# An mLSTM cell and a leaky-ReLU feed-forward on one core: the first chunk's order of work written anew, weight quarters loaded in four transfers

## The chip, the cores and the metric

The kernel runs on one core of a Trainium2 chip. A core has five engines that run side by side and wait for one another by semaphores: TensorE (PE; its weight loads are listed as PEld), VectorE (DVE), ScalarE (ACT), GpSimd (POOL) and SyncE (SP), which issues nearly all transfers (DMAs). Each engine works through its own queue in order. The metric is device time in microseconds, lower is better.

## The reference

```python
# mLSTM cell: 4 batches, 8 heads, 768 steps, head size 40
for t in range(S):
    m_new = np.maximum(f[t] + m, i[t])
    f_stab, i_stab = np.exp(f[t] + m - m_new), np.exp(i[t] - m_new); m = m_new
    C = f_stab * C + i_stab * einsum('bhd,bhe->bhde', v[t], k[t])
    n = f_stab * n + i_stab * k[t]
    h = einsum('bhde,bhe->bhd', C, q[t]); nq = einsum('bhd,bhd->bh', n, q[t])
    y[t] = sigmoid(o[t]) * h / np.maximum(np.abs(nq), 1)
# feed-forward: x is y as (3072, 320); w_in (320, 2048), w_out (2048, 320)
h = x @ w_in
out = np.maximum(0.01 * h, h) @ w_out
```

The inputs of the cell are float32. w_in and w_out come as float64, 8 bytes an element.

## The kernel before

**Tiling.** The 768 steps are cut into 6 chunks of 128. A chunk has one item for each of the 4 batches, so items ("s") count from 0 to 23, and items 0 to 3 are the first chunk. Inside a chunk the recurrence is written as products: the gates become running sums (`gates`), a matrix of decays w for each head (mask by `spread_first`, exponential by `prep_exp`), scores k·q by `u_scores`, and the values by `u_values`; the state at a chunk's end comes from `state`. The feed-forward of a chunk (512 tokens) starts when its cell is done and runs beside the next chunk's cell.

**The first chunk.** It has no earlier state and no earlier feed-forward to run beside. An item passes through: loads of k, q, v (`load`) and o (`load_o`), transposes of k and q by TensorE into PSUM and a copy by ScalarE (`u_transpose`), scores, multiplication by w on VectorE, the state product, which needs v scaled by GpSimd (`prep_vu`), and its copy on VectorE (`u_state`), values, denominators and gate on VectorE with a last product on GpSimd (`gate`), transposes of the result and five copies on ScalarE (`u_x`), which place it for the feed-forward. `prepare_step` is three memsets on GpSimd that ready the item's state tile for the next chunk.

**The weights.** w_in is loaded in four quarters (`load_weights` 0 to 3), each as float64 words into a raw area, and narrowed to float32 by `narrow_weights`: one step on ScalarE (L247) and six on VectorE (L249 to L263). w_out follows in eight pieces. Each quarter's 320 rows are kept in five slots of 64 rows, in two halves: row half r = 0 in partitions 0 to 63, r = 1 in 64 to 127, and `SLOTS` says which 64 rows stand in which slot. The halves use different slot orders, so that the products of a feed-forward half (`half` in `ff_units`) run in pairs on different rows of TensorE.

**What sets the order.** The whole program is traced with TensorE, VectorE, ScalarE and GpSimd in the order in which the code calls the operations; SP's transfers come out in program order here too. `first_chunk` is written out by hand: it calls the steps of items 0 to 3 one after the other, and with them two halves of the first feed-forward (`ffs[0]`, `ffs[1]`: tokens of items 0 and 1). After it a few more loads are issued (items 4 and 5, weights, items 6 and 7), and a loop runs the rest: the remaining feed-forward halves, between them the units of the next chunk's cell at fixed places. In the loop's first turn `ahead(4)` puts item 4's transposes (`u_split`, tiles tk, L534) on TensorE, which need its k and q, and then `ffs[2]`, which needs the tokens of items 2 and 3. Below, "ff 0", "ff 1" and "ff 2" are the first three halves, "q 4" is q of item 4.

**PSUM.** Two pools of four banks each: `psf` (feed-forward, masks, and the warming products) and `psc` (everything else of the cell). A new tile waits until a bank of its pool is read out.

**Warming.** `warm(14)` issues 14 products of the identity with itself on TensorE at the start. Nothing reads them.

Of the kernel before, what the change touches and what calls it, by code (L numbers as in the profile page):

```python
# [18 lines left out]
def kernel(  # L19
# [184 lines left out]
    def load_weights(n):  # L204

        m = n - QN
        if n < QN:
            dst = w_in[:, n, :]
        else:
            dst = w_out[:, 2 * m : 2 * m + 2, :].rearrange("p a d -> p (a d)")  # L210
        to = dst
        if wide:
            if n < 2:
                at = NF * GT - 2 * WC * (n + 1)
                raw = acts_l[:, at : at + 2 * WC].bitcast(U64)
            elif n < QN:
                raw = raw_t[:, WC * (n - 2) : WC * (n - 1)]
            elif m < 2:
                raw = w_out[:].rearrange("p f d -> p (f d)")[:, (2 + m) * WC : (3 + m) * WC].bitcast(U64)
            else:  # L220
                at = (4, 0, 1, 2, 3, 4)[m - 2] * HW
                raw = raw_t[:, at : at + HW]
            raws[n] = (raw, dst)
            to = raw
        if n < QN:
            src = moe_w_in[:, n * QC : (n + 1) * QC].rearrange("(k p) (r c) -> r p k c", p=DP, r=2)
            for slot in range(KC):
                for r in range(2):
                    nc.sync.dma_start(
                        to[DP * r : DP * (r + 1), 2 * P * slot : 2 * P * (slot + 1)], src[r, :, SLOTS[r][slot], :],  # L230
                    )
        else:
            rows = moe_w_out[2 * m * P : 2 * (m + 1) * P, :]
            nc.sync.dma_start(to.rearrange("p (a d) -> p a d", d=Dm), rows.rearrange("(a p) d -> p a d", p=P))
# [190 lines left out]
    def spread_first(a, s2):  # L425


        ab = [psf.tile([P, 2, H // RG, P], F32, name=f"ab{r}", tag="mm") for r in range(RG)]
        for n in range(2):
            for m in range(H // RG):  # L430
                for r in range(RG):
                    bh = (s2 + n) * H + m * RG + r
                    rows = ts(r, BH)
                    nc.tensor.matmul(
                        ab[r][:, n, m, :], lhsT=ident[rows, r * BH + bh : r * BH + bh + 1].to_broadcast([BH, P]),
                        rhs=a[rows, :], start=True, stop=True,
                    )
        for n in range(2):
            w = st[s2 + n]["w"] = wk.tile([P, H, P], F32, name="w", bufs=NL)
            for r in range(RG):  # L440
                nc.vector.tensor_tensor(
                    w[:, r::RG, :], ab[r][:, n], cmask[:].unsqueeze(1).to_broadcast([P, H // RG, P]), op=ALU.add,
                )
# [98 lines left out]
    def u_transpose(s):  # L542
        d = st[s]
        d["kqT"] = wk.tile([P, 2, PR * P], F32, name="kqT")
        for i in range(2):
            tp = psc.tile([P, PR, P], F32, name="tkq", tag="c")
            for j in range(PR):
                nc.tensor.transpose(  # L548
                    tp[:, j, :], d["kq"[i]][:, 2 * j : 2 * j + 2, :].rearrange("p h d -> p (h d)"), ident[:],
                )  # L550
            nc.scalar.copy(d["kqT"][:, i], tp[:].rearrange("p j t -> p (j t)"))

    def u_scores(s):
        d = st[s]
        kqT, w = d["kqT"], d["w"]
        sc = [psc.tile([P, PR, P], F32, name=f"sc{r}", tag="c") for r in range(2)]
        for j in range(PR):
            for r in range(2):
# [3 lines left out]
                )  # L562
        for r in range(2):
            nc.vector.tensor_tensor(w[:, r::2, :], w[:, r::2, :], sc[r][:], op=ALU.mult)
# [62 lines left out]
    def u_state(s):  # L627
        state(s)
        state_copy(s)

# [6 lines left out]
    def u_values(s):  # L637
        d = st[s]
        pa = d["pa"] = psc.tile([P, H, D1], F32, name="pa", tag="c")
        for h in range(H):  # L640
            nc.tensor.matmul(pa[:, h, :], lhsT=d["w"][:, h, :], rhs=d["va"][:, h, :D1], start=True, stop=True)  # L641
        d["den"] = wk.tile([P, H], F32, name="den")
        denominators(d["den"][:], pa[:, :, D])

    def gate(s):
# [7 lines left out]
        )  # L653
        nc.gpsimd.tensor_tensor(x3, x3, d["den"][:].unsqueeze(2).to_broadcast([P, H, D]), op=ALU.mult)
# [78 lines left out]
    def u_x(s):  # L733
# [3 lines left out]
        if b == 0:  # L737
            st["xT", c] = wk.tile([P, KC, GT], F32, name="xT", bufs=1)
        xT = st["xT", c]
        xt = psc.tile([P, KF + 1, P], F32, name="xt", tag="c")  # L740
        for kk in range(KF):
            nc.tensor.transpose(xt[:, kk, :], d["x"][:, ts(kk, P)], ident[:])
        nc.tensor.transpose(xt[:KR, KF, :], d["x"][:, KF * P :], ident[:])
        tok = ts(b, P)
# [5 lines left out]
        del st[s]  # L750
# [149 lines left out]
    def cell_units(c):  # L900
        if c == 1:
            units = [(fn, c * B + n) for n in range(B) for fn in (u_parts, u_plain)]
            units.insert(2 * B - 2, (u_gates, c + 1))
            return units + [(u_x, s) for s in range(B, 2 * B)]
# [39 lines left out]

    def first_chunk():

        for n in range(B):
            load(n)
        load_o(0)
        load_o(1)  # L950
        load_weights(0)
        load_o(2)
        load_o(3)
        for n in range(1, 3):
            load_weights(n)
        gates(0)
        gates_exp(0)
        warm(14)
        bu, a, _ = bus[0]
        gates_T(0, bu)  # L960
        u_transpose(0)
        spread_first(a, 0)
        run(prep_exp(0))
        prep_vu(0)
        prep_vu(1)
        prepare_tiles()
        u_transpose(1)
        u_scores(0)
        u_state(0)
        run(prep_exp(1))  # L970
        spread_first(a, 2)
        gates(1)
        gates_exp(1)
        u_scores(1)
        u_values(0)
        u_state(1)
        u_transpose(2)
        prep_o(0)
        gate(0)
        run(prep_exp(2))  # L980
        prep_vu(2)
        w = narrow_weights(0)
        next(w, None)
        u_values(1)
        u_gates(1)
        u_scores(2)
        prep_o(1)
        gate(1)
        u_state(2)
        for _ in w:  # L990
            pass
        u_transpose(3)
        run(prep_exp(3))
        prep_vu(3)
        prepare_step(0)
        prepare_step(1)
        u_x(0)
        u_values(2)
        u_scores(3)
        u_x(1)  # L1000
        u_state(3)
        prep_o(2)
        gate(2)
        w = narrow_weights(1)
        for _ in range(4):
            next(w, None)
        ffs = ff_units(0)
        ffs[0]()
        u_values(3)
        prep_o(3)  # L1010
        gate(3)
        u_x(2)
        ffs[1]()
        for _ in w:
            pass
        u_x(3)
        prepare_step(2)
        prepare_step(3)
        return ffs

    E = mybir.EngineType
    with tc.manual_schedule(engines={E.PE, E.DVE, E.Activation, E.Pool}):
        ffs = first_chunk()
        for s in (B, B + 1):
            feed(s)
            for i in range(1, 3):
                load_late(s, i)
            if s == B:
                load_weights(3)
        for n in range(3):  # L1030
            load_weights(QN + n)
        for s in (B + 2, B + 3):
            feed(s)


        ffs = ffs[2:]
# [98 lines left out]
```

## Time and profile before

| | |
|---|---|
| median of 3 runs | 509.8 us (506.64 to 511.63) |
| the profiled execution, span | 508.0 us; what lies around the span isn't recorded |
| PE busy in the span | 492.0 us (97%) |
| DVE, ACT, POOL busy | 308.1, 171.5, 137.7 us |
| first chunk: last transposes of its results on PE | 49.18 to 49.7 us |
| mean granted clock | 0.983 |

The page cuts the span into 40 slices of 12.7 us. A digit is the busy share of an engine in tenths, and PEclk the granted TensorE clock in tenths of full speed. A line of the timeline reads: start, duration, engine, line of the kernel, operation, output<-inputs, count, and in brackets the idle time before it and what ended it. "SPq" is SP's queue: the time is that of issuing. A DMA in the chain of work has the time from its issue to its landing. In a table of windows a row gives a stretch, its length, each engine's busy time with a count of instructions (PE, PEld, DVE, ACT, POOL), the granted clock, the DMA engines' busy share and GB/s.

### The profile page before, as it was taken

The numbers are of one execution on the slowest core, as the hardware profiler recorded it, in microseconds if no ns is written. First come the engines' busy times: TensorE is split into PE (matmuls) and PEld (weight loads), VectorE is DVE, ScalarE is ACT, GpSimd is POOL, SyncE is SP. The second block draws the span as 40 slices with busy tenths as digits, with TensorE's granted clock in tenths as the row PEclk, the third lists the DMA queues.
The fourth block names the chain that finished last, engine by engine and source line by source line (L and its number), as shares of the span: only waits on it lengthen the run. The fifth ranks groups of instructions, "written<-read, shape, count | busy, mean of one in ns | idle before, by whom it ended". The sixth has DMA issues, their size and how long they took to land.

```text
span 508.0 us, 12526 instructions
## 1 busy us (share of the span) xinstructions
PE 492.0 (97%) x4981; PEld 366.6 (72%) x4981; DVE 308.1 (61%) x515; ACT 171.5 (34%) x478; POOL 137.7 (27%) x175
## 2 busy tenths in 40 slices
PE   8878999999999999999999999999899999999997
PEld 7766878767655489955589855599755599744797
DVE  4779898899954778635765826764825664101321
ACT  3664864652722510323411323311213411022210
POOL 4243443360402404413104614014612003000020
PEclk9877999999999999999999999999999999999999
DMA  9977687888765551565663566564466212200001
GB/s 116 146 204 154 149 219 185 168 152 175 155 145 87 131 124 46 133 130 144 147 132 92 115 137 170 137 141 97 109 135 177 68 53 62 69 1 1 1 1 52
DMA packets 165290, 59.21 MB, mean 117 GB/s; under 512 B 128816, under 2 KB 156016, under 8 KB 165232
## 3 DMA queue, kind: packets, MB, share of 16 engines
q1 hardware_dynamic: 164848, 58.28, 52.2%
q8 instruction: 39, 0.64, 0.5%
q14 instruction: 19, 0.16, 0.1%
q10 hardware_dynamic: 384, 0.13, 0.1%
HBM read 51.68 MB, written 6.70 MB: 115 GB/s over the span
## 4 chain that ended last, share of the span: by engine, by line
PE 79%; DVE 9%; DMA 3%; ACT 3%; POOL 2%; issue 2%; SPq 2%; ACTq 0%; POOLq 0%; DVEq 0%
PE ph L759 36%; PE po L835 26%; PE po L794 6%; PE pT L695 3%; PE sd L614 3%; SPq L359 1%; PE sd L619 1%; DMA S<-in_v_dram 1%; ACT kqT L540 1%; PE tkq L548 1%; DVE raw L261 1%; DMA rb<-in_q_dram 1%; DMA w<-a_dr 1%; PE pa L641 1%; DVE qn L511 1%
## 5 line engine op out<-in xcount | busy, mean ns | idle before, releaser
L759 PE MATMUL ph<-xT,w_in 64*128 64x512 f32 (+1 forms) x1120 | 216.2, 538 | 2.4 <-DVE y L887 1.4
L759 PEld LDWEIGHTS ph<-xT,w_in 64*128 64x128 f32 x1120 | 108.6, 189 | 95.1 <-issue 86.3
L767 ACT ACTIVATE acts<-ph 128x512 f32<-128x512 f32 (+1 forms) x112 | 53.9, 533 | 179.0 <-PE ph L759 178.9
L835 PEld LDWEIGHTS po<-w_out,acts 128*128 128x128 f32 x640 | 87.3, 190 | 3.8 <-issue 3.8
L835 PE MATMUL po<-w_out,acts 128*128 128x160 f32 x640 | 89.1, 300 | 0.0
L450 POOL TENSOR_TENSOR w<-w,i 128x512 f32<-128x512 f32 x20 | 26.9, 1345 | 117.3 <-DMA w<-a_dr 117.2
L624 DVE TENSOR_TENSOR qn<-w,sd 64x512 f32<-64x512 f32 x40 | 27.4, 684 | 40.2 <-PE sd L619 20.5
L458 ACT ACTIVATE w<-w,gT 128x64 f32<-128x64 f32 (+1 forms) x192 | 50.8, 348 | 2.7 <-POOL w L450 1.7
L592 POOL TENSOR_TENSOR S<-S,f 40x336 f32<-40x336 f32 x36 | 32.0, 889 | 67.3 <-PE pT L695 36.3
L835 PE MATMUL po<-raw,acts 128*128 128x160 f32 x320 | 45.5, 300 | 0.0
L835 PEld LDWEIGHTS po<-raw,acts 128*128 128x128 f32 x320 | 43.9, 190 | 0.3
L794 PE MATMUL po<-w_out,acts 128*128 128x320 f32 x128 | 36.5, 436 | 0.0
L702 DVE STREAM_TRANSPOSE hb<-pT 128x512 f32<-128x512 f32 x16 | 11.5, 717 | 31.0 <-PE pT L695 30.8
L794 PEld LDWEIGHTS po<-w_out,acts 128*128 128x128 f32 x128 | 23.6, 190 | 9.3 <-issue 0.3
L511 DVE TENSOR_TENSOR qn<-kqT,ea 64x512 f32<-64x512 f32 x32 | 28.4, 888 | 1.0
L709 POOL TENSOR_TENSOR xb<-xb,den 128x320 f32<-128x320 f32 x16 | 11.7, 729 | 56.8 <-DVE xb L706 56.6
L596 DVE TENSOR_TENSOR S<-S,sd 40x336 f32<-40x336 f32 x36 | 18.1, 503 | 12.1 <-POOL S L592 11.2
L614 PEld LDWEIGHTS sd<-kqT 40*64 40x64 f32 x640 | 19.9, 135 | 6.1 <-issue 6.1
L822 DVE TENSOR_TENSOR raw<-acts 128x1024 f32<-128x1024 f32 x10 | 11.8, 1222 | 18.3 <-ACT acts L767 18.2
L713 DVE STREAM_TRANSPOSE x<-xb 128x512 f32<-128x512 f32 x16 | 18.2, 1140 | 7.6 <-POOL xb L709 7.6
L835 PE MATMUL po<-raw 128*128 128x160 f32 x160 | 22.5, 299 | 0.0
L835 PEld LDWEIGHTS po<-raw 128*128 128x128 f32 x160 | 22.0, 190 | 0.0
(151 smaller groups left out, 551.8 us busy)
## 6 DMA issues: line engine op xcount, KB each, us to landing
w<-a_dr SPq DMA_DIRECT2D x40, 128.0 KB
rb<-in_k_dram SPq DMA_DIRECT2D x64, 80.0 KB
rb<-in_q_dram SPq DMA_DIRECT2D x64, 80.0 KB
rb<-in_o_gate_dram SPq DMA_DIRECT2D x64, 80.0 KB
ea<-a_dr SPq DMA_DIRECT2D x32, 128.0 KB
kn<-in_k_dram SPq DMA_DIRECT2D x24, 160.0 KB
raw<-in_moe_w_out_dram SPq DMA_DIRECT2D x6, 640.0 KB
S<-in_v_dram SPq DMA_DIRECT2D x80, 40.0 KB
```

The lines of the kernel that those rows point to most:

```text
L450: nc.gpsimd.tensor_tensor(w, w, cm2.unsqueeze(1).to_broadcast([P, H, SL]), op=ALU.add)
L458: yield nc.scalar.activation(w[:, h, :], w[:, h, :], AF.Exp, bias=gT[c][:, 0, bh : bh + 1], scale=1.0)
L511: nc.vector.tensor_tensor(mixed(s)[rows, 1 - r], d["kqT"][rows, 1].rearrange("p (h t) -> p h t", t=SL), d["ea"][rows], op=ALU.mult,)
L592: nc.gpsimd.tensor_tensor(new, old, g, op=ALU.mult)
L596: nc.vector.tensor_tensor(new, new, st[s]["dC", u], op=ALU.add)
L614: nc.tensor.matmul(bank[1 - u][toks, h, :], lhsT=kqT[rows, 0, ts(h, SL)], rhs=kqT[rows, 1, ts(h, SL)], start=True, stop=True,)
L624: nc.vector.tensor_tensor(mixed(s)[toks, u], w[toks], bank[1 - u][toks], op=ALU.mult)
L713: nc.vector.transpose(in_blocks(xq[:]), xb[:].rearrange("p (j n) d -> p j n d", n=TB))
L759: nc.tensor.matmul(ph[r][:, cols], lhsT=w_row(r, slot, j), rhs=xT[DP * r : DP * (r + 1), slot, cols], start=(slot == 0), stop=(slot == KC ...
L767: nc.scalar.activation(acts[:, f, cols], ph[r][:, cols], AF.Prelu, alpha=0.01)
L794: nc.tensor.matmul(po[n][:], lhsT=acts[:, f, ts(n, P)], rhs=w_out[:, f, :], start=(f == 0), stop=(f == NF - 1),)
L835: nc.tensor.matmul(bank[:], lhsT=left[:, f, :], rhs=right[:, f, :], start=f == 0, stop=f == KH - 1)
```

## The change

1. `first_chunk` no longer calls the steps in Python order. A string `ORDER` lists them, 131 entries with the transfers, and a loop runs them. To let parts of a step stand apart, helpers are split: `u_transpose` (one set at a time) and `transpose_copy`, `u_scores` and `scores_mix`, `spread_first` and `spread_mask`, `state` and `state_copy`, `u_values` and `values_den`, `gate` and `gate_scale`, `u_x` and `x_copy`. The operations are the same ones.
2. The transfers are in that list too. Weight quarter 0 (`lw 0`) goes ahead of item 3's k, q, v (`ld 3`), o of item 3 (`lo 3`) behind quarter 2. The loads of items 4 to 7 (`fd`), of q and o of items 4 and 5 (`ll`), and of weights 3 to 6 are in the list; o of item 4 goes ahead of q of item 4, and q and o of item 5 behind weights 3 to 5 and item 6.
3. The warming products are 9 and not 14; `idle n` adds n products of the same kind further on, 14 in all, into a PSUM tile of their own (`warmer`).
4. A quarter of w_in is loaded by four transfers and not ten: for each half, one of three slots and one of two.

```diff
-            for slot in range(KC):
-                for r in range(2):
+            for r in range(2):
+                at = 0
+                while at < KC:
+                    k0, m = run_of(r, at)
                     nc.sync.dma_start(
-                        to[DP * r : DP * (r + 1), 2 * P * slot : 2 * P * (slot + 1)], src[r, :, SLOTS[r][slot], :],
+                        to[DP * r : DP * (r + 1), 2 * P * at : 2 * P * (at + m)].rearrange("p (k c) -> p k c", k=m),
+                        src[r, :, k0 : k0 + 2 * m - 1 : 2, :],
                     )
+                    at += m
...
+    def warmer():
+        st["warm"] = psf.tile([P, P], F32, name="warm", tag="mm")
+
+    def idle(n):
+        for _ in range(n):
+            nc.tensor.matmul(st["warm"][:], lhsT=ident[:], rhs=ident[:], start=True, stop=True)
+
+    ORDER = """
+warm 9; g 0; ld 0; ge 0; ld 1; tr 0 0; ld 2; tr 0 1
+ug 0; lo 0; tc 0 1; ab 0; abw 0; tr 1 0; tr 1 1; lo 1
+lw 0; vu 0; tc 0 0; vu 1; exp 0; tc 1 1; abw 1; ld 3
+exp 1; lo 2; warmer; sc 0; tiles; st 0; lw 1; scm 0
+stc 0; tc 1 0; ab 2; val 0; st 1; g 1; abw 3; abw 2
+sc 1; o 0; lw 2; ge 1; idle 2; idle 1; stc 1; o 1
+scm 1; idle 3; tr 2 0; tc 2 0; lo 3; tr 2 1; nw 0; tc 2 1
+ug 1; nw 0; val 1; vu 3; den 0; gate 0; vu 2; gate 1
+sc 2; tr 3 0; nw 0; exp 2; den 1; scm 2; ps 0; st 2
+gp 0; exp 3; tc 3 0; tr 3 1; x 0; tc 3 1; idle 4; sc 3
+nw 0; gp 1; stc 2; xc 0; x 1; nw 0; val 2; nw 0
+o 2; nw 0; st 3; scm 3; xc 1; nw 1; gate 2; nw 1
+ff 0; o 3; val 3; den 2; nw 1; ps 1; fd 4; gp 2
+stc 3; den 3; gate 3; ll 4 2; ll 4 1; ps 2; gp 3; nw 1
+x 2; xc 2; ps 3; fd 5; ff 1; lw 3; nw 1; lw 4
+x 3; lw 5; nw 1; fd 6; ll 5 1; xc 3; ll 5 2; lw 6
+idle 4; nw 1; fd 7
+"""
...
+            "ld": load, "lo": load_o, "lw": load_weights, "g": gates, "ge": gates_exp, "warm": warm,
+            "ug": lambda c: gates_T(c, bus[c][0] if c == 0 else bus.pop(c)[0]),
+            "tr": u_transpose, "tc": transpose_copy, "ab": lambda n: spread_first(bus[0][1], n), "abw": spread_mask,
+            "exp": lambda n: run(prep_exp(n)), "vu": prep_vu, "tiles": prepare_tiles, "sc": u_scores, "scm": scores_mix,
+            "st": state, "stc": state_copy, "val": u_values, "den": values_den, "o": prep_o, "gate": gate,
+            "gp": gate_scale, "nw": step, "ps": prepare_step, "x": u_x, "xc": x_copy, "ff": ff,
+            "warmer": warmer, "idle": idle, "fd": feed, "ll": load_late,
```

## The prediction

> **What bounds the kernel now.** I read the page's slices first, then the windows by stage, then the timelines of TensorE and of the transfer queue, then the chain.
>
> ```profile
> PE   8878999999999999999999999999899999999997
> PEclk9877999999999999999999999999999999999999
> DMA  9977687888765551565663566564466212200001
> ```
>
> From the fifth slice on (50 us) PE is busy nearly throughout at the full clock. Only the first four slices, which are the first chunk, have idle PE and a reduced clock. So whatever moves the start of the steady stage moves the end by about as much. That start is the third half of the first feed-forward (ff 2), at 51.64 us:
>
> ```profile
> 38.33 0.79 PE L572 MATMUL dC<-vu,kn 128*40 128x42 f32 x16 [1.80 <-ACT xT L749]
> 39.77 4.64 PE L759 MATMUL ph<-xT,w_in 64*128 64x256 f32 x20 [0.66 <-DVE w_in L263]
> 46.82 2.43 PE L759 MATMUL ph<-xT,w_in 64*128 64x256 f32 x20
> 50.62 0.25 PE L534 MATMUL tk<-ident,rb 64*40 64x64 f32 x2 [0.65 <-DMA rb<-in_q_dram]
> 51.64 4.59 PE L759 MATMUL ph<-xT,w_in 64*128 64x256 f32 x40
> ```
>
> ff 0 waits until 39.77 for the last narrowing step of weight quarter 0 (L263), and takes 4.64 us where ff 1 takes 2.43. Then PE waits 0.65 us for q of the next chunk's batch 4. The windows show the clock (after the colon: length, PE busy, ..., granted clock, DMA share, GB/s):
>
> ```profile
> 17.51:20.93 3.42, 1.84 (x29) 1.50 (x28) 3.35 (x12) 0.97 (x4) 0.00 (x0) 1.00 0.83 132
> 24.35:31.17 6.82, 6.69 (x52) 6.07 (x51) 2.48 (x8) 3.05 (x7) 0.87 (x3) 0.50 0.72 179
> 34.59:37.99 3.40, 0.68 (x7) 0.28 (x3) 3.33 (x3) 2.65 (x10) 2.32 (x5) 1.00 0.62 199
> 41.41:44.82 3.41, 3.41 (x19) 2.33 (x15) 3.27 (x7) 0.38 (x2) 1.14 (x1) 0.50 0.65 126
> ```
>
> After a stretch with PE 54% busy (17.51) and one with 20% (34.59) the clock is 0.50, until a stretch is full.
>
> The transfer queue (SP), and q's own landing in the chain:
>
> ```profile
> 18.77 7.75 SPq L229 DMA_DIRECT2D acts<-in_moe_w_in_dram  x10
> 27.83 6.58 SPq L229 DMA_DIRECT2D acts<-in_moe_w_in_dram  x10
> 34.45 6.35 SPq L229 DMA_DIRECT2D raw<-in_moe_w_in_dram  x10
> 46.77 3.46 DMA rb<-in_q_dram
> ```
>
> The three quarters that are fetched before q 4 take 20.7 us of SP, and q 4 lands at 46.77 + 3.46 = 50.2.
>
> **The change, part by part.**
>
> *Transfers.* A quarter is 128 x 1280 x 8 bytes = 1.31 MB. Issued as ten it moves at an issue each 0.64 us. As four, SP issues it in about 4 x 0.64 = 2.6 us, so the transfers' own rate decides. The trace has no such transfer, and these are the nearest rows:
>
> ```profile
> 29.70:31.50 1.80, 1.79 (x9) 1.48 (x9) 0.92 (x3) 1.72 (x4) 0.03 (x1) 0.59 0.89 255
> 34.40:40.90 6.50, 2.78 (x33) 2.06 (x31) 6.30 (x9) 4.83 (x12) 2.46 (x6) 0.78 0.65 208
> 65.40:67.70 2.30, 2.30 (x24) 1.84 (x20) 2.23 (x3) 0.66 (x2) 1.24 (x1) 1.00 0.93 298
> ```
>
> At 29.7 pieces of w_in that were issued earlier run off a backlog, at 255 GB/s: 5.1 us a quarter. At 34.4 they come at the pace of the issues, 208 GB/s: 6.3. At 65.4 w_out comes in 128-partition transfers of 0.66 MB with rows of 2.5 KB, 298 GB/s and the best to hope for: 4.4. At the bad end, if a transfer to 64 partitions gets half of that, 149 GB/s: 8.8. I take 5.1, from the row with the same packets and a queue behind them. Then three quarters take 15.3 us, and 0.6 for one late issue such as SP shows now and then, 15.9 in place of 20.7: 4.8 saved. The o of batch 4 now goes ahead of q 4: one issue, 0.6 us. q 4 lands at 50.2 - 4.8 + 0.6 = 46.0. From its landing to ff 2 are 51.64 - 50.24 = 1.4 us (the rest of the tk transposes), so **by the transfers ff 2 starts at 47.4**.
>
> A rule of the Trainium skill speaks against this part. The Trainium skill, page "SBUF — State Buffer", section "Door 1: The DMA port swizzle", says that 64 neighbouring partitions reach only 8 of the 16 DMA ports, about 218 GB/s at best. By that, the new order, which fills one half of the partitions with two transfers and then the other (ten transfers alternated), takes 6.0 us a quarter, an estimate from the page's figure, and q 4 lands at 48.7. The 255 GB/s row alternates halves and so doesn't refute it.
>
> *The order.* Quarter 0 moves ahead of batch 3's k, q and v. It lands at 29.1 now: the narrowing's first step on ACT (L247) starts at 29.12 after a wait for it. Three transfers of 160 KB leave its front, at SP's pace of 1.18 us each, and it takes 5.7 instead of 7.75 itself: 29.1 - 3.5 - 2.1 = 23.5. Batch 1's v lands at 12.55; five transfers (k, q, v 2, o 0, o 1) later it is 18.5, then come quarter 0 (5.7) and k, q, v 3 (3.5): v 3 lands at 27.7, some 7 us later than now. On ACT that first step now stands ahead of batch 2's second transpose copy and of exp 2 and 3: they wait with it for the quarter, from 21.7, and exp 3 is done at 30.4, before anything asks for it.
>
> To find where that leads I went down each engine's new queue with the rows' durations, every step at the later of its engine's end and its last input. PE: transposes 0.5 us a set, scores 1.14, state 0.46, values 1.85, x 0.4, ff half 2.38; a spare is two passes of 0.107 (four 128-wide weight loads of tkq take 0.42). DVE: mask 1.37, mix 1.28, gate 0.49, narrowing 0.83 + 1.24 + 1.50 + 0.87 + 1.50 + 1.49. ACT: exp 2.45, x copies 1.66. POOL: vu 0.95, product 0.74, step memsets 1.08. The same walk down the old queues, with the granted clock, ends at 49.6; in the trace the last x transposes run from 49.18 to 49.7.
>
> Until 18.8 us old and new are alike, since both wait for k, q and v. Nine warming products instead of fourteen end at 5.3, and PE then waits for k till about 6.7: nothing lost, unless the clock rises 3.4 us later for it (0.6 at most). The six spares at 18.8 to 20.1 fill the wait of 1.58 us after which the old clock fell. Then POOL binds: its queue has vu 3 ahead of vu 2, and vu 3 needs v 3. So 27.7 + 0.95 + 0.95 = 29.6, state 2 follows on PE after 2.3 us without work, then memsets 1.08 and the product 0.74, and x 0 starts at 31.6. From there PE has, with no gap over 0.1, x 0.4, four spares 0.86, scores 1.14, x 0.4, values 1.85, state 0.46, ff 0 2.38, values 1.85, x 0.4, ff 1 2.38, x 0.4, four spares 0.86: 13.4 us, end **45.0**, against 49.7. ff 0 falls at 36.7, just where quarter 0's narrowing ends on DVE (36.6). The last x copies end on ACT at 46.3 (51.5 now), quarter 1's narrowing on DVE at 48.2 (51.8).
>
> No spare stands in the gap ahead of state 2. By the 54% row such a gap lets the clock fall for one or two stretches of 3.4 us; at a pace of 0.53 (ff 0's 2.43 to 4.64) the walk then ends 0.4 or 1.9 us later, the x copies at 46.7 or 48.2. The Trainium skill, page "TensorE: Matmul & The Clock Gate", section "What's actually happening", has the clock fall after at least one idle window of 3.4 us; by that the gap would cost nothing. The row at 17.51 shows a fall after a window that was half busy, and the row decides.
>
> *Sum.* ff 2 starts at the later of 47.4 (q 4) and 46.4 to 48.3 (x copies). I take 47.7, 3.9 us before 51.64. Splitting the helpers in two adds no instruction. The spares' 14 x 0.214 = 3.0 us of PE are counted: 1.3 in an old wait, 0.9 within the 13.4 on the path, the last 0.9 beside the wait for q 4 and the x copies. With that cover gone they cost 0.9 more.
>
> What is late next: DVE, which waits 1.2 us for ACT at 52.98 now, moves along. q of batch 5 now stands behind w_in quarter 3, two of w_out and two batches' k, v and w (4.4 us each on SP): 42.5 + 4.4 + 5.1 + 4.2 + 4.4 + 3.5 = 64.1, and is needed at 68.8 - 3.9 = 64.9. That hides it by 0.8 us; at slower quarters its lateness adds to PE.
>
> The profiled execution spans 508.0, no more is shown around it; the median of the runs is 509.8, 1.8 above. 508.0 - 3.9 = 504.1 on its account, **506.0** on the median's.
>
> **The rivals.**
>
> *Quick quarters.* At 4.4 us three take 13.8, q 4 lands at 43.9 and no longer decides; v 3 comes 0.7 us earlier, the x copies end at 45.6. If the clock holds, ff 2 starts at 45.7, 5.9 earlier: 503.9. For it: 298 GB/s. Against: 64 partitions, not 128.
>
> *Half the partitions bind.* At no better than the 208 GB/s row, 6.3 us, three take 19.5, q 4 lands at 49.6, ff 2 starts at 51.0. PE then has 2 to 3 us without work ahead of tk, and perhaps a stretch at 0.50 behind it (1.6 us): between 0.6 gained and 1.0 lost, 509 to 511. The Trainium skill's 6.0 would give ff 2 at 50.1, 508.3.
>
> *Slower than before.* At 149 GB/s, 8.8 us, three take 27.0, q 4 lands at 57.1, ff 2 starts at 58.5: 6.9 lost, 517. The loss begins at 6.9 us a quarter. Against it: the small ones reach 208 GB/s into the same halves.
>
> *It doesn't keep the clock.* With the old stretches at 0.50 the walk ends at 48.4 on PE and 49.7 on ACT, ff 2 starts at 50.0: 1.6 gained, 508.2. For it: the gap ahead of state 2.
>
> **How the numbers follow.** Forecast (504.7 to 507.5) 0.40; quick 0.27; half the partitions 0.18; slower 0.08; clock 0.07. 1% of the time is 5.1 us, about what a measurement can tell from no change. Faster by over 1% (under 504.7) is the quick case and the forecast's low edge: 0.34. Slower by over 1% is the slow case, and a little of the half-partition one with q 5 late as well: 0.10. The rest is 0.56. The range leaves out the slow case and the outer edges of the others: 502.8 to 511.0.
>
> **What would show it.** SP's w_in rows at 2.6 to 5 us a quarter; ACT's first step of narrowing near 23.5; POOL's vu 3 near 27.7 after a wait for v; ff 0 near 36.7, in 2.4 us; the last x near 44; tk's wait for q 4; ff 2 near 47.7. The forecast is wrong if quarters take over 6 us, if the wait for q 4 is over 2 us or gone, if POOL's vu isn't what state 2 waits for, or if the steady stage gives the gain back in waits for w_in quarter 3, q 5 or DVE.

## The result, and the profile after

| | before | after | ratio |
|---|---|---|---|
| median of 20 runs each | 510.33 us | 513.5 us | 1.006 [1.004, 1.008] |
| profiled execution, span | 508.0 us | 512.0 us | |

The changed kernel is slower by 0.6%, 3.2 us by the medians. The forecast was a gain, to 506.0 us, with a range from 502.8 to 511.0. A "mark" below is the start of a piece of work on TensorE (PE) in the profiled execution.

The slices of the page, after:

```profile
PE   6876989999999999999999999999799999999997
PEclk9979799999999999999999999999999999999999
DMA  9999887788653551565664467664466312100001
```

The DMA row is now 9 in each of the first four slices, and the clock has a low slice of its own at the fifth (51 to 64 us), where before the steady stage was already running at full clock. The timeline of PE, after (the lines that answer to those of before; start, duration, then in brackets the wait):

```profile
28.05 2.08 PE L570 MATMUL sc<-kqT 40*128 40x128 f32 x16 [3.60 <-ACT kqT L561]
...
38.48 2.43 PE L785 MATMUL ph<-xT,w_in 64*128 64x256 f32 x20 [0.18 <-DVE w_in L267]
...
46.84 0.44 PE L757 MATMUL xt<-ident,x 128*128 128x128 f32 x2 [1.22 <-POOL x L672]
51.73 0.33 PE L541 MATMUL tk<-ident,rb 64*40 64x64 f32 x2 [3.20 <-DMA rb<-in_q_dram]
53.59 8.57 PE L785 MATMUL ph<-xT,w_in 64*128 64x256 f32 x60
...
73.40 0.25 PE L541 MATMUL tk<-ident,rb 64*40 64x64 f32 x2 [1.31 <-DMA rb<-in_q_dram]
```

The first chunk did get shorter: its last transposes start at 46.84 and not 49.18. But behind them PE waits 3.20 us for q 4 (0.65 before), so ff 2 starts at 53.59 and not 51.64. The 60 products from its start on take 8.57 us; in a run below, at full clock, they take 6.75. Then comes a new wait of 1.31 us for q 5, ahead of the next item's transposes (tk again). The windows, after (length, PE, PEld, DVE, ACT, POOL busy, granted clock, DMA share, GB/s):

```profile
23.20:26.60 3.40, 1.25 (x12) 1.13 (x11) 0.00 (x0) 0.42 (x1) 0.00 (x0) 1.00 1.02 107
...
30.00:40.00 10.00, 9.77 (x102) 8.65 (x102) 9.76 (x15) 8.72 (x24) 5.84 (x9) 0.83 1.07 213
44.00:47.00 3.00, 1.78 (x17) 1.27 (x14) 2.65 (x3) 2.46 (x8) 2.05 (x2) 1.00 0.35 34
47.07:50.48 3.41, 1.45 (x15) 1.18 (x13) 3.34 (x3) 2.96 (x6) 1.85 (x4) 1.00 0.82 176
50.48:53.88 3.40, 2.15 (x62) 2.00 (x64) 3.27 (x4) 0.21 (x2) 3.22 (x3) 0.50 0.86 103
53.88:57.29 3.41, 3.41 (x18) 2.71 (x18) 3.34 (x6) 2.91 (x7) 2.19 (x2) 0.50 0.64 193
```

After each of the two waits (PE busy 1.25 and 1.45 of 3.4 us) the clock is at 0.50 for two stretches. From 30 to 40 the weights arrive at 213 GB/s with the DMA engines all busy; from 44 to 47, just before q 4 is issued, the DMA engines are busy for a third of the time. SP's queue tells why (the time is that of issuing):

```profile
19.35 6.03 SPq L358 DMA_DIRECT2D S<-in_v_dram  x1
...
27.05 2.56 SPq L231 DMA_DIRECT2D acts<-in_moe_w_in_dram  x4
...
36.65 9.27 SPq L363 DMA_DIRECT2D S<-in_v_dram  x4
...
47.90 0.58 SPq L386 DMA_DIRECT2D rb<-in_q_dram  x1
...
58.74 9.88 SPq L363 DMA_DIRECT2D S<-in_v_dram  x4
...
69.98 0.59 SPq L386 DMA_DIRECT2D rb<-in_q_dram  x1
```

SP does issue a quarter in 2.56 us. But an issue behind the quarters, usually 0.6 us, then takes 6.03 (v 3), 9.27 for four (v 4) and 9.88 for four (v 6). These holds end shortly after the last packet of the weights that were issued ahead: at 25.38 for v 3, where quarter 0's last 2 KB packet ends at 24.92; at 42.55 for the first issue of v 4, where quarter 2's ends at 42.10; at 66.73 for the third of v 6, where w_out's ends at 66.42. q 4 is issued at 47.90, later than before (46.77), and q 5 at 69.98; it lands 3.38 later, at 73.36, by the chain of work.

What happens at 26 to 28 us, all engines, after:

```profile
26.18 1.35 ACT L251 ACTIVATE w_in<-acts 128x1280 f32<-128x1280 f32 x1 [4.51 <-DMA acts<-in_moe_w_in_dram]
...
27.42 0.58 ACT L561 COPY kqT<-tkq 128x512 f32<-128x512 f32 x1
27.56 0.83 DVE L253 TENSOR_SCALAR w_in<-w_in 128x1280 f32<-128x1280 f32 x1 [4.59 <-ACT w_in L251]
...
28.05 0.80 PE L570 MATMUL sc<-kqT 40*128 40x128 f32 x4 [3.60 <-ACT kqT L561]
28.10 0.86 POOL L475 TENSOR_TENSOR vu<-S,gT 128x320 f32<-128x320 f32 x1 [13.44 <-DMA S<-in_v_dram]
```

ACT stands 4.51 us at quarter 0's first narrowing step. The copy of item 2's second transposes is behind it, so item 2's scores wait 3.60 us on PE, and DVE stands 4.59 us at its own narrowing step. One late transfer stops three engines. The first chunk's end hangs on another one: in the chain of work o 3 is issued at 33.51, behind quarters 1 and 2, and lands 10.29 us later, and the gate and the transposes of item 3 follow it.

The lag of after behind before, by marks: 1.95 us at ff 2, 3.3 at the fifth half, 4.5 at the ninth (74.4 for 69.9), 2.5 at the first product with w_out (98.5 for 96.0; before loses some of that stretch itself, with waits of 0.94 and 0.70 at 75.40 and 77.30), still 2.5 at 291.5, and 3.95 at 443.7, after a wait for VectorE's y near 369 of 2.60 us where before has one of 1.40. For this last 1.5 us I found no cause in the first chunk; the wait is between 0.2 and 1.7 in the other profiles that show it.

### The profile page after: what moved, and what is told of

Same layout as the page of the kernel before. It is cut to its first block, busy times and chain, and to the rows that moved or that the text cites. A ratio compares the mean times of both kernels' runs of the same rounds, so it can differ in the third digit from the quotient of the medians.

```text
span 512.0 us, 12529 instructions
## 1 busy us (share of the span) xinstructions
PE 491.3 (96%) x4999; PEld 367.3 (72%) x4999; DVE 309.0 (60%) x515; ACT 171.9 (34%) x478; POOL 141.2 (28%) x175
## 4 chain that ended last, share of the span: by engine, by line
PE 77%; SPq 9%; DMA 5%; DVE 4%; ACT 2%; issue 1%; POOL 1%; ACTq 0%; POOLq 0%; DVEq 0%
PE ph L785 37%; PE po L861 26%; PE po L820 6%; PE pT L713 3%; SPq L363 3%; PE sd L627 3%; SPq L358 3%; DMA acts<-in_o_gate_dram 2%; SPq L231 2%; DMA acts<-in_moe_w_in_dram 1%; PE sd L632 1%; SPq L372 1%; SPq L417 1%; DMA w<-a_dr 1%; DMA rb<-in_q_dram 1%
## 5 line engine op out<-in xcount | busy, mean ns | idle before, releaser
L785 PEld LDWEIGHTS ph<-xT,w_in 64*128 64x128 f32 x1120 | 109.9, 189 | 94.1 <-issue 83.0
L605 POOL TENSOR_TENSOR S<-S,f 40x336 f32<-40x336 f32 x36 | 32.3, 898 | 79.1 <-PE pT L713 38.0
L609 DVE TENSOR_TENSOR S<-S,sd 40x336 f32<-40x336 f32 x36 | 18.1, 503 | 13.5 <-POOL S L605 12.5
```

Source lines behind the costliest of these rows:

```text
L605: nc.gpsimd.tensor_tensor(new, old, g, op=ALU.mult)
L609: nc.vector.tensor_tensor(new, new, st[s]["dC", u], op=ALU.add)
L785: nc.tensor.matmul(ph[r][:, cols], lhsT=w_row(r, slot, j), rhs=xT[DP * r : DP * (r + 1), slot, cols], start=(slot == 0), stop=(slot == KC ...
```

## The experiments

Ratios are to the kernel before, run beside each kernel; its medians there were 509.74 to 510.59 us.

| kernel | median us | ratio | ff 2 at | first w_out product at |
|---|---|---|---|---|
| before | 510.33 | 1 | 51.6 | 96.0 |
| after | 513.5 | 1.006 [1.004, 1.008] | 53.6 | 98.5 |
| four transfers alone | 507.46 | 0.9963 [0.9931, 0.9995] | 50.2 | 95.0 |
| four, halves in turn, alone | 506.98 | 0.9938 [0.991, 0.9966] | 50.2 | 94.6 |
| order alone, ten transfers | 514.06 | 1.0086 [1.0052, 1.012] | 54.2 | 99.4 |
| after, no spares | 512.72 | 1.0031 [0.9998, 1.0064] | 51.8 | 98.4 |
| after, q 4 early | 514.9 | 1.0089 [1.0056, 1.0122] | 49.7 | 100.9 |
| after, wait for q 4 filled | 514.68 | 1.0091 [1.0057, 1.0124] | 52.8 | 100.1 |
| after, q 4 and q 5 early | 511.48 | 1.0027 [0.9997, 1.0056] | 49.2 | 97.0 |
| after, narrowing out of the way | 513.22 | 1.0067 [1.0039, 1.0095] | 52.8 | 100.4 |
| after, both of these | 510.07 | 1.0008 [0.9978, 1.0038] | 52.4 | 96.1 |
| and o 3, quarter 3 early | 510.15 | 0.9983 [0.9957, 1.0008] | 48.9 | 95.8 |
| and halves in turn | 511.96 | 0.9996 [0.9962, 1.003] | 47.8 | 93.0 |
| and no spares | 509.49 | 0.9981 [0.9954, 1.0008] | 51.3 | 98.8 |
| after, halves in turn | 511.91 | 1.0035 [1.0004, 1.0066] | 51.3 | 95.4 |
| o 3, quarter 3 early, less VectorE work | 508.69 | 0.9967 [0.9938, 0.9997] | 47.1 | 94.4 |
| before, less VectorE work | 510.36 | 0.9991 [0.9965, 1.0018] | 51.4 | 93.3 |

The "spares" are the products of `idle`. A line that begins with "and" adds to the line above it. The two last columns are of one profiled execution each. For the order alone, and for the two kernels of the new order with halves in turn and spares, that was the fastest of the twelve (511.8, 507.7 and 505.8 us), and for the wait that is filled the fastest of seven (513.65), so their marks are early for their medians.

**The two parts apart.** In the kernel before, only the loop over ten transfers is replaced by the four of the changed kernel:

> The kernel before with the four transfers a quarter as its only edit. Theory A (halves and queue): a transfer to 64 partitions moves at some 218 GB/s, 6.0 us a quarter, its 2 KB packets take 0.16 us instead of 0.08; that is little better than ten transfers at SP's pace (6.4 to 7.7), so q 4 lands between 48 and 51 us and the time is 509 to 512 (before: 510.3). Theory B (the new order of the compute queues is what costs): no loss here, 508 to 510. Theory C (the spare products cost their 3.0 us): no spares in this kernel, 510.3.

And the changed kernel with the ten transfers put back:

```diff
-            for r in range(2):
-                at = 0
-                while at < KC:
...
+            for slot in range(KC):
+                for r in range(2):
+                    nc.sync.dma_start(
+                        to[DP * r : DP * (r + 1), 2 * P * slot : 2 * P * (slot + 1)], src[r, :, SLOTS[r][slot], :],
+                    )
```

> The changed kernel with ten transfers a quarter again, the new order and the spares kept. Theory A: packets of 0.08 us again, but SP needs 6.4 us for each of the three quarters ahead of q 4 and one more issue for o 4, so q 4 lands near 51 either way; PE waits some 3 us for it and runs at half clock after the wait: 511 to 513.5. Theories B and C: nothing of the cause is touched, 513.5.

The four transfers alone win 0.4%, under the times of all three theories; the order alone loses 0.9%, a little over theory A's. So the loss is the order's, and the four transfers are the better half of the change. The order loses on another path with ten transfers: in that profile PE doesn't wait for q 4, as theory A had it. It waits 2.08 us at 26.44 for the copy that stands behind quarter 0's narrowing, the clock is then 0.50 until 47.1, and the last transposes of the first chunk start at 51.82; q 5 costs 1.12 us at 72.84. How little the four transfers win is in the records of w_in's 2 KB packets before 45 us, and in the windows of ten microseconds in which quarters 1 and 2 arrive:

| kernel | median packet | GB/s in that window | DMA share |
|---|---|---|---|
| before (ten transfers) | 84 ns | 207 (31 to 41) | 0.66 |
| after (four) | 165 ns | 213 (30 to 40) | 1.07 |
| four alone | 166 ns | 208 (31 to 41) | 1.06 |
| after, halves in turn | 156 ns | 222 (29 to 39) | 1.06 |
| halves in turn alone | 156 ns | 225 (30 to 40) | 1.07 |

Ten transfers leave the DMA engines a third idle, held by SP's issues. Four fill them, but each packet then takes twice as long, and the sum hardly moves. By the first and the last of their 2 KB packets, quarters 1 and 2 together run from 28.60 to 42.10 in the trace of after, 6.7 us each; the last of them share the DMA engines with the small packets of o 3 and k 4. Before, they run from 29.71 to 42.63, 6.5 each.

**Is it the half of the partitions?** The four transfers of a quarter are issued lower, upper, lower, upper half, and not two to one half and then two to the other; first in the changed kernel, then in the kernel before:

```diff
+            runs = []
             for r in range(2):
                 at = 0
                 while at < KC:
                     k0, m = run_of(r, at)
+                    runs.append((r, at, k0, m))
...
+            for i in (0, 3, 1, 2):
+                r, at, k0, m = runs[i]
+                nc.sync.dma_start(
...
```

> The changed kernel with the four transfers of a quarter issued in turn to the lower and the upper half of the partitions (three slots, three slots, two, two) and not two to one half and then two to the other. Theory 'half the partitions bind': neighbouring transfers overlap in the queue, so both halves are written at once for part of the time: packets of 2 KB take less than 0.16 us, a quarter 5.1 to 5.6 us in place of 6.0, the time 0.5 to 1.5 us shorter than the changed kernel's. Theory 'four transfers are slow by themselves' (size or shape of the transfer): packets stay at 0.16 to 0.17 us and a quarter at 6.0, the time as the changed kernel's.

> The kernel before, with only the ten transfers of a quarter replaced by four in turn to the two halves. Four, two to one half and then two to the other, gave 507.46. Theory 'half the partitions bind': 506.5 to 507.3, packets of 2 KB at 0.155 us. Theory 'issues alone counted': 507.5, as with the other four.

Packets fall from 165 to 156 ns and the rate rises from 213 to 222 GB/s, with the same bytes, sizes and number of transfers. In the kernel before it rises from 208 to 225. So which half a transfer writes to does matter, as the first theory said, with a gain of 4 and 8% in the rate, at the low end of what it said or under it. Most of the doubling stays: the ten transfers, in turn as well, had 84 ns. That a large transfer is slow by itself doesn't explain it: the transfers of w_out are larger (0.66 MB) and go to all 128 partitions, and their 2.5 KB packets take 107 ns from 63 to 66 us in the trace of after. So the half of the partitions is the likely bound, and the shape of the transfers isn't ruled out. The changed kernel's median goes to 511.91 and the four alone to 506.98; by the intervals, neither is apart from the same kernel without the halves in turn. Halves in turn in the order of before has the lowest median of all these kernels, 0.6% under before.

**q 4 early.** The changed kernel with q of batch 4 ahead of weight quarter 2, and nothing else moved:

```diff
-sc 1; o 0; lw 2; ge 1; idle 2; idle 1; stc 1; o 1
+sc 1; o 0; ll 4 1; lw 2; ge 1; idle 2; idle 1; stc 1; o 1
...
-stc 3; den 3; gate 3; ll 4 2; ll 4 1; ps 2; gp 3; nw 1
+stc 3; den 3; gate 3; ll 4 2; ps 2; gp 3; nw 1
```

> The changed kernel with one transfer moved: q 4 ahead of weight quarter 2, not behind it, o 4 and batch 4's k, v and w. Theory A: q 4 lands before 40 us, PE no longer waits for it and keeps its clock; ff 2 starts when the last x copies are done, 49.2 to 50 instead of 53.6: 508 to 510. Theory B: the chunk's own order decides, 512.5 to 513.5. Theory C: 513.5.

The timeline of PE in this run:

```profile
49.66 4.59 PE L785 MATMUL ph<-xT,w_in 64*128 64x256 f32 x40
...
73.30 0.33 PE L541 MATMUL tk<-ident,rb 64*40 64x64 f32 x2 [4.28 <-DMA rb<-in_q_dram]
```

ff 2 starts 2 us earlier than before, at full clock, as theory A expected. All of it is given back in one wait: q 5 is used at 73.30, and was at 73.40 in the changed kernel. The time of 514.9 is over what each theory expected. The fall of the clock has moved with the wait: from 68.24 to 71.65 PE is busy for 0.78 of 3.41 us, and from 71.65 to 78.47 the clock is 0.50, where the changed kernel has it at 1.00. So the first product with w_out comes 2.3 us later than there, though both leave the wait at the same time.

**The wait for q 4 filled.** The changed kernel with 15 spare products more, in the wait for q 4:

```diff
-idle 4; nw 1; fd 7
+idle 19; nw 1; fd 7
```

> The changed kernel with 15 spare products more (19 for 4) ahead of the tk transposes, 3.2 us of them in TensorE's wait of 3.20 us for q 4. If the half clock from 50.5 to 57.3 is the price of that wait, it goes, and 60 passes from ff 2 on take 6.8 us for 8.6: 511.5 to 512.3 in place of 513.5. If the clock falls all the same, the time stays or grows by up to 1 us.

The timeline of PE:

```profile
52.81 6.75 PE L785 MATMUL ph<-xT,w_in 64*128 64x256 f32 x60
...
73.32 0.25 PE L541 MATMUL tk<-ident,rb 64*40 64x64 f32 x2 [3.83 <-DMA rb<-in_q_dram]
```

From ff 2 on the clock holds, and 60 products take 6.75 us for 8.57, so the half clock was the price of that wait. Still nothing is won, and neither expectation on the time held: the next tk waits until 73.32, for 3.83 us, and behind it the clock is 0.50 from 74.15 to 77.56. Three kernels that reach this place between 49.66 and 53.59 all leave it at 73.3 to 73.4. Up to there, the date of q 5's landing sets the pace.

**q 5 early as well.** The edit of q 4 early, and q and o of batch 5 ahead of weight quarter 3, as in the kernel before:

```diff
-x 2; xc 2; ps 3; fd 5; ff 1; lw 3; nw 1; lw 4
-x 3; lw 5; nw 1; fd 6; ll 5 1; xc 3; ll 5 2; lw 6
+x 2; xc 2; ps 3; fd 5; ll 5 1; ll 5 2; ff 1; lw 3; nw 1; lw 4
+x 3; lw 5; nw 1; fd 6; xc 3; lw 6
```

> The changed kernel with q 4 issued ahead of weight quarter 2, and q 5 and o 5 ahead of weight quarter 3 (as in the kernel before); the computing order stays. Theory 'transfer order' (the loss is q 4 and q 5 standing behind weights): ff 2 at 49.5 to 50, no wait of TensorE for q 5 near 73, the rest as long as before, so 1.5 to 2 us under the kernel before: 507.5 to 509. Theory 'blocked narrowing' (the loss is the first narrowing step holding up ScalarE, VectorE and TensorE near 26): that wait is still there with the half clock after it, and the time stays at 511 or more. Theory 'weights become late in turn': quarter 3 or w_out lands later, TensorE waits for them between 70 and 95, time 512 or more.

PE no longer waits for q 5. By the medians 3.4 us come off the kernel with q 4 early alone, whose interval only touches this one, and 2.0 off the changed kernel, whose interval overlaps with it. The third theory's mechanism comes up with it. PE, and then ACT, in this run:

```profile
66.57 2.02 PE L785 MATMUL ph<-xT,w_in 64*128 64x256 f32 x12 [3.27 <-ACT acts L793]
```

```profile
64.89 1.35 ACT L251 ACTIVATE w_in<-raw 128x1280 f32<-128x1280 f32 x1 [5.82 <-DMA raw<-in_moe_w_in_dram]
```

Now quarter 3 is late (its narrowing starts at 64.89, before at 61.35), ACT stands 5.82 us at its first narrowing step, and the feed-forward's copies out of PSUM stand behind it. PE waits 3.27 us for them, and the clock is 0.50 from 67.97 to 71.39. The time lies between that theory's (512 or more) and that of the transfer order (507.5 to 509).

**Narrowing out of the way.** The changed kernel with the steps of narrowing moved behind item 2's copies, exponential and mix, and v 2 scaled ahead of v 3; then this together with both q early:

```diff
-scm 1; idle 3; tr 2 0; tc 2 0; lo 3; tr 2 1; nw 0; tc 2 1
-ug 1; nw 0; val 1; vu 3; den 0; gate 0; vu 2; gate 1
-sc 2; tr 3 0; nw 0; exp 2; den 1; scm 2; ps 0; st 2
-gp 0; exp 3; tc 3 0; tr 3 1; x 0; tc 3 1; idle 4; sc 3
+scm 1; idle 3; tr 2 0; tc 2 0; lo 3; tr 2 1; tc 2 1
+ug 1; val 1; vu 2; den 0; gate 0; gate 1
+sc 2; gp 0; vu 3; tr 3 0; exp 2; nw 0; den 1; scm 2; nw 0; ps 0; st 2
+nw 0; exp 3; tc 3 0; tr 3 1; x 0; tc 3 1; idle 4; sc 3
```

> The changed kernel with the first narrowing step of quarter 0 behind item 2's copies and exponential, VectorE's steps of it behind item 2's mix, and v of item 2 scaled ahead of v of item 3; the transfers stay. Theory 'transfer order': item 2's scores come near 24.5 and the last x transposes 2 to 3 us earlier, but ff 2 still waits for q 4 (landing 51.4) and starts near 53, and the wait for q 5 near 73 stays: 512.5 to 514.5. Theory 'blocked narrowing': at least 2 us are won, 510 to 511.5.

> Both edits of the two kernels before it at once: q 4 and q 5 early, narrowing out of the way. Theory 'transfer order': about as the one with q 4 and q 5 early alone, less at most what the first x transposes come earlier, with ff 2 at 48.5 to 49.5: 506.5 to 508.5. Theory 'blocked narrowing': clearly under the one with q 4 and q 5 early alone, by 2 us or more.

Item 2's scores come at 24.53 and not 28.05, ff 0 at 36.0 and not 38.48; the time stays at 513.22, for tk still waits 3.45 us for q 4 and 3.46 for q 5. With both edits it is 510.07: over the 506.5 to 508.5 of theory 'transfer order', apart from the changed kernel by its interval, and 0.2% under the one with q 4 and q 5 early, with overlapping intervals. So the loss of 3 us goes with these two edits. By the medians the larger part of it is the transfers' order (2.0 us), and the blocked engines cost little as long as a transfer is later still; by the intervals, the division isn't shown. The next late one shows on PE in the run with both:

```profile
47.96 0.69 PE L757 MATMUL xt<-ident,x 128*128 128x128 f32 x2 [4.82 <-POOL x L672]
```

It is the gate of item 3, which needs o 3: ACT waited for it until 44.94, 6.31 us.

**o 3 and quarter 3 early too.** On top of both edits:

```diff
-sc 1; o 0; ll 4 1; lw 2; ge 1; idle 2; idle 1; stc 1; o 1
-scm 1; idle 3; tr 2 0; tc 2 0; lo 3; tr 2 1; tc 2 1
+sc 1; o 0; lo 3; ll 4 1; lw 2; ge 1; idle 2; idle 1; stc 1; o 1
+scm 1; idle 3; tr 2 0; tc 2 0; tr 2 1; tc 2 1
...
-stc 3; den 3; gate 3; ll 4 2; ps 2; gp 3; nw 1
-x 2; xc 2; ps 3; fd 5; ll 5 1; ll 5 2; ff 1; lw 3; nw 1; lw 4
+stc 3; den 3; gate 3; ll 4 2; lw 3; ps 2; gp 3; nw 1
+x 2; xc 2; ps 3; fd 5; ll 5 1; ll 5 2; ff 1; nw 1; lw 4
```

> The two edits together (q 4, q 5 and o 5 early, narrowing out of the way), and now also o of item 3 ahead of weight quarter 2 and weight quarter 3 ahead of item 5's loads. Theory 'a queue of transfers, each needed one at its date': TensorE's wait for the gate of item 3 near 48 (4.82 us in the run before) goes, the last x transposes come at 43 to 44.5, ff 2 at 46.5 to 48, quarter 3's narrowing starts by 62, and the steady stage keeps the gain: 504.5 to 507. Theory 'the steady stage takes it back' (whatever starts earlier waits for later weights or for VectorE): ff 2 comes at 47 to 48, but the first product with w_out stays at 95.5 to 97 and the time at 509 to 511.

Then with the halves in turn, and that without the 14 spares:

> The kernel of the line before with a quarter's four transfers issued in turn to the two halves of the partitions. In the run that did this to the changed kernel 2 KB packets took about 0.156 us in place of 0.166 and the time fell by 1.6 us. Theory 'queue': 0.5 to 1 us less than the line before. Theory 'steady stage takes it back': the same time.

> The kernel with o 3 early and alternating halves, without the 14 spare products. If the spares keep the clock up, TensorE falls to half clock in one or two more stretches and the time is 1 to 2 us longer. If they only fill waits that the clock ignores or take path time: the same within 0.6 us, or 0.9 shorter.

No late transfer is left that holds PE up to 73 us in the first of the three. ff 2 starts at 48.86, 2.8 us earlier than before, and the first product with w_out at 95.8, 0.2 earlier; the time is what "the steady stage takes it back" expected. PE's timeline shows the place, and the windows who is busy there:

```profile
73.65 1.09 PE L527 MATMUL tq<-ident,y 64*40 64x64 f32 x32 [1.97 <-POOL y L494]
75.55 0.30 PE L632 MATMUL sd<-S,vu 64*40 64x42 f32 x3 [0.69 <-POOL vu L485]
```

```profile
60.00:66.00 6.00, 6.00 (x80) 5.20 (x76) 5.87 (x7) 3.06 (x11) 2.20 (x1) 1.00 0.94 231
66.00:72.00 6.00, 5.68 (x110) 4.75 (x106) 5.80 (x9) 4.82 (x13) 2.52 (x3) 1.00 0.77 155
...
75.88:79.29 3.41, 3.41 (x67) 2.94 (x59) 2.09 (x5) 0.56 (x3) 1.42 (x1) 0.50 0.58 56
```

DVE is busy 5.8 to 5.9 of each 6 us from 54 to 72, as it was before. y is GpSimd's, behind a product that waits for DVE's gate, and that stands behind quarter 3's narrowing. DVE's last step of quarter 3 starts at 71.38, against 73.12 before: PE came 2.8 us earlier, DVE 1.7. So these two waits take 2.66 us where before's take 1.64: 1.0 of the 2.8 us goes there. Another 1.6 goes to the clock. Behind the waits (PE busy for 1.54 of 3.41 us) it is 0.50 from 75.88 to 79.29; PE is still 1.75 us ahead of before at 75.55, and 0.16 at the first product with w_out. In the profile with the halves in turn the waits are the same (1.82 and 0.69), the clock holds, and PE stays 3.0 us ahead up to that product (93.02 for 95.98).

That profile is the fastest execution of its kernel; the median with the halves in turn is no lower (511.96). Without spares the time isn't apart from that either; from 20.6 to 44.4 the clock is 0.50, with the spares only from 18.7 to 22.1 and from 25.5 to 32.3. In these profiles they do keep the clock, and the times show nothing won by it.

**Is VectorE the bound there?** The last three VectorE steps of narrowing are left out for quarters 2 and 3 (the low word isn't added), in the kernel with o 3 early and, as control, in the kernel before:

```diff
+        if n in (2, 3):
+            yield
+            yield
+            return
         nc.vector.tensor_scalar(hi, d, scalar1=0xFF800000, scalar2=None, op0=ALU.bitwise_and)
```

> The kernel with o 3 early and four transfers (510.15), with the last three VectorE steps of narrowing left out for weight quarters 2 and 3 (the low word is not added, so the weights of these quarters keep some 20 bits): 8.2 us less VectorE work between 52 and 75. Theory 'VectorE takes the place as the bound there' (97% busy from 48 to 72 in that kernel): the wait of TensorE for GpSimd's y near 73.6 goes, the first product with w_out comes at 93 to 94, and the time falls by 2 to 3.5 us, to 506.5 to 508. Theory 'TensorE is bound there as before, the rest is the clock': within 0.8 us of 510.15.

> The kernel before with the same steps left out (low word of quarters 2 and 3 not added). It is the control: if VectorE's work there costs the kernel before nothing, since its TensorE is full from 54 to 72, the time stays within 1 us of the kernel before. If it falls by as much as in the other kernel, VectorE was the bound of that stage before the change too, and an earlier ff 2 could never have been worth its whole 3.9 us.

508.69 us against 510.15 in the first, 510.36 against 510.59 for the kernel before in the control. PE's wait for y goes in both, and GpSimd's product y takes 0.72 us where it took 1.97 beside the narrowing. The 1.5 us against 0.2 lean to VectorE, but the intervals overlap and the first is short of its 2 to 3.5. In it PE waits 1.80 us at 82.93 for the next q, and the clock is 0.50 from 83.05 to 86.46 behind that. In the control's profile the first product with w_out comes 2.7 us earlier than before, so VectorE's work there did hold the kernel before too; that profile (511.71 us) is one of the control's slowest, with a stretch at 0.50 from 366.9 to 370.3, and the median shows nothing of the 2.7. That VectorE takes part of the gain is likely, and not shown.

**The spares in the changed kernel.** All 14 `idle` products are left out of the order:

> The changed kernel without the 14 spare products. Theory A: they lie in waits, so taking them out gains at most 0.9 us and may cost clock after 18.7 us; q 4 still decides: 513 to 515. Theory C: 3.0 us come back, 510.5. Theory B: 513.

0.8 us less than the changed kernel, with overlapping intervals, and under the 513 of theories A and B. Here too the clock is low for longer (20.4 to 44.3), ff 2 comes earlier than with them (51.8), and tk waits 2.25 us for q 5 at 71.76.

## Why the prediction was wrong

That q 4 decides ff 2's start was right. What failed is the step *Transfers*, the time of a quarter above all, and behind it the dates of q 4 and q 5.

- **A quarter at 5.1 us.** The sum has 10.2 us for quarters 1 and 2. From the first packet to the last they take 13.5, and took 12.9 as ten transfers, and the last weight packet ends at 42.10, at 42.63 before: of the 4.8 us that were to be saved, 0.5 was. The row that was chosen, 255 GB/s, was of packets left over from a backlog; in after the weights come at 213. The rival that speaks of half the partitions, with 6.0 to 6.3, was nearest, and had 0.18. Its mechanism is supported by packets of 165 ns for 84 at a full DMA share, and by the 4 to 8% in rate that issuing the halves in turn wins. The Trainium skill, page "SBUF — State Buffer", section "Door 1: The DMA port swizzle", gives 218 GB/s for 64 neighbouring partitions; the trace has 213 with two transfers to one half after another, and 222 to 225 with halves in turn. By the sum itself a loss begins at 6.5 us a quarter (20.7 = 3 x 6.5 + 0.6 + 0.6), not at the 6.9 that stands with the slow rival; with 6.7 it gives q 4 at 50.8 and ff 2 at 52.2.
- **q 4 lands at 46.0:** it is used at 51.73, 5.7 us later, after 3.20 us of waiting. Up to v 3 the walk was right (28.10 for 27.7). The two quarters behind it make 3.3 us of the error, and they start 0.5 after v 3. The next 1.4 are a term that the sum doesn't have. It made SP's issue time a matter of count (2.6 us a quarter, and it is 2.56), and let q 4 follow as closely behind the weights as before. In the trace SP is held at v 4 until 42.55, with the weights moved; it still has three issues of v 4, two transfers of w and o 4 to make, and meanwhile the DMA engines run mostly empty (35% busy, 34 GB/s from 44 to 47). From the last weight packet to the use of q 4 are 9.6 us, 7.6 before, and the sum had 0.6 of that for o 4. The half-partition rival's 49.6 for q 4 lacks the same term, and its 509 to 511 with it.
- **q 5 lands at 64.1, hidden by 0.8 us:** it lands at 73.36. Of these 9.3 us 5.4 come with q 4, which is issued at 47.90 and not 42.5. Most of the rest is quarter 3 and the two transfers of w_out, 12.5 us from the first packet to the last for 9.3 in the sum; SP stands 9.88 at v 6 behind them. The sum named this wait as what is late next at slower quarters, and gave it no time. It mattered most: with ff 2 at 49.66 the kernel still took 514.9, with q 5 early as well 511.48.
- **Quarter 0 lands at 23.5, and what stands behind it is done "before anything asks for it":** its last packet ends at 24.92, its narrowing starts at 26.18, and item 2's second copy is asked for at 24.45. The gap of PE is there in the walk, 2.3 us ahead of state 2 for want of v; in the trace it is 3.60, ahead of scores 2. The place was wrong, and its size by 1.3. ff 0, at 36.7 in the walk, is at 38.48, and the last x, near 44, at 46.84; the walk has no wait for o 3.
- **The clock falls after the gap, against the Trainium skill's idle window** (page "TensorE: Matmul & The Clock Gate", section "What's actually happening"): right, and twice, after windows with PE 1.25 and 1.45 of 3.4 us busy; each time for two stretches. The forecast had priced the first, and the second only in a rival, with 1.6 us; it is 8.57 for 6.75, 1.8. That it lasts "until a stretch is full" was misread: the row at 24.35 is two stretches long, PE is busy for 6.69 of its 6.82 us, and the clock is 0.50 to its end.
- **The spares, 3.0 us:** without them the time is 0.8 less, not apart from nothing.
- **DVE "moves along":** where ff 2 starts 2.8 us earlier, DVE's narrowing of quarter 3 ends 1.7 earlier, and PE waits 1.0 us more for what stands behind it. So even with q 4 and q 5 in time, some 1 us of ff 2's gain of 3.9 wasn't to be had, and each new wait can cost the clock besides.
- **ff 2's start moves the end:** in the kernel before's own order the direction is right (four alone: ff 2 1.4 earlier, median 2.6 less), and the size isn't explained. In the new order it fails, as soon as a later transfer has a date of its own.

The slow rival (a transfer to 64 partitions at 149 GB/s) named the right sign and the wrong mechanism: the loss isn't in the rate, which stays about the same (207 GB/s before, 213 after).

## What to carry to other kernels

When the transfers of a queue are reordered, write down for every one of them the time at which it is needed and the time at which it lands, to the end of the stage, and not only for the first one on the path: here each late one that was repaired (q 4, q 5, o 3, quarter 3) only showed the next. Price an issue by what is still outstanding ahead of it on the queue, not by its count alone. A wait that is filled or removed can move on, with its fall of the clock, to the next late transfer. And put nothing that waits for a large transfer ahead of short work on an in-order engine, unless that transfer is sure to have landed.

## What the runs showed of the hardware that wasn't expected

- SP's issues are cheap until enough is outstanding, and then it stands: 0.6 us becomes 6.03 for one behind quarter 0, and 9.27 and 9.88 for four behind quarters 1 and 2 and behind quarter 3 and w_out. The long holds end 0.3 to 0.5 us after the last weight packet. In the order with ten transfers no issue takes over 2.2 us up to 75 us. At the end of the two longest holds the DMA engines are busy for only 35 and 40% of 3 us (44 to 47, 67 to 70). What SP waits for, the bytes, the packets or the transfers outstanding, isn't shown.
- GpSimd's product y takes 1.97 us beside VectorE's narrowing and 0.72 without it, in the new order and in the old one.
- The clock doesn't come back after one full stretch. In the order with ten transfers it stays at 0.50 from 26.6 to 47.1, through stretches in which PE is recorded as busy throughout (the columns are those of the windows above):

```profile
33.44:36.85 3.41, 3.41 (x24) 3.13 (x23) 3.34 (x3) 2.07 (x6) 1.25 (x2) 0.50 0.63 212
...
43.67:47.09 3.42, 3.42 (x18) 2.38 (x14) 0.82 (x3) 0.58 (x3) 1.69 (x4) 0.50 0.50 77
47.09:50.50 3.41, 3.41 (x31) 3.08 (x33) 1.61 (x5) 1.80 (x6) 0.57 (x1) 1.00 1.08 187
```

Nor does the busy share alone tell when it falls: in the changed kernel not after 43.66 to 47.07 (2.19 of 3.41 busy), in the one with o 3 early after 31.50 to 34.90 (2.52 of 3.40). What the clock counts can't be read from the busy time of these records; it stays open.
